# Attention stream: parts of q and k transposed by the DMA engines instead of TensorE, value products grouped by pairs of heads, one block placed earlier

## The chip, the cores and the metric

The kernel runs on one core of a Trainium2 chip. Its time is the device time of one execution in microseconds (us), and the figure compared is the median of several runs. PE is TensorE, ACT is ScalarE, DVE is VectorE, POOL is GpSimd and SP is SyncE, whose queue issues almost all transfers here.

## The reference

```python
# attention: 8 batches, 12 heads, 448 positions, head dimension 64
scores = scale * np.matmul(q, k.transpose(0, 1, 3, 2)) - np.log(S)
attn = 1.0 / (1.0 + np.exp(-scores))
attn_out = np.matmul(attn, v).astype(np.float32)
...
# feed-forward: x is 3584 tokens x 768; w_in is 768 x 2048, w_out is 2048 x 768
x = np.ascontiguousarray(attn_out.transpose(0, 2, 1, 3)).reshape(B * S, H * D)
h = x @ w_in
g = h - np.tanh(h)
return (g @ w_out).astype(np.float32)
```

All inputs are float32. The weights arrive in the kernel as 64-bit words and are converted on the chip.

## The kernel before

A batch of 448 tokens goes through three steps: attention for its 6 pairs of heads, the first product with `w_in` (`moe1`), and the second product with `w_out` (`moe2`). To get float32 accuracy from float16 matmuls, an operand is split into a high and a low float16 part, each with a power-of-two scale, and three products (high·high, high·low, low·high) are summed in PSUM.

Batch 0 is done first with plain float32 matmuls while the weights are loaded and converted. After that attention is a stream (`stream`), a generator that yields one *block* at a time, and the driver `second` places blocks between the steps of a batch's second product. A step is 6 matmuls (`yield 980`), so a batch's second product has 48 steps and 16 half-size ones for the remaining 64 tokens, counted to 56. The tables `BLOCKS0` (batch 0), `BLOCKS1` (batch 1) and `BLOCKS` (later batches) say after which step a block is issued. `ALONE` is the index of the block in `BLOCKS` that completes the next batch's attention. Three, five and seven steps after it come the scales of the next batch's `x` and its splitting into `xhl` (`batch_scales`), which the next `moe1` reads. The first product has no blocks in it.

A pair of heads `g` takes two blocks, `i = 0` and `i = 1`, and each treats two of the four chunks of 112 keys. Before the change a block issues on PE, in this order:

- `i = 0`: four float32 transposes of pair g+1's q through PSUM (`turn`, tile `qT`); `i = 1`: four of pair g+2's k (`turn_k`, tile `kT`) and one small matmul for the sums of squares (line 316);
- 12 score matmuls (line 362), two chunks x three products x two heads;
- 12 products with v (line 386), for the two chunks of the block before (`do_av`).

ACT takes the sigmoid (line 371) and makes the high part of the weights (line 377), DVE the low part (line 378). `parts` splits the transposed q or k, read from PSUM, into `Q` or `K` (lines 337, 339, 340): ACT writes the high part of q, DVE that of k for most pairs, and DVE writes the low part of both. `norms` (line 308) takes sums of squares of a later pair on ACT. The pairs of batch 1 do the v product in float32 instead (`av32`, `AV32 = 2`).

PE, ACT, DVE and POOL run in the order in which the code is written. SP's transfers are placed by the framework's scheduler; SP issues them in order, and each waits there until its source is written and its destination is free. Tiles come from rotating buffers: `K` and `Q` have two buffers each, and so have the loaded `kn` and `qn`.

Of the kernel before, what the change touches and what calls it, by code (L numbers as in the profile page):

```python
# [8 lines left out]
F16 = mybir.dt.float16  # L9
BF16 = mybir.dt.bfloat16  # L10
F32 = mybir.dt.float32
# [3 lines left out]
AF = mybir.ActivationFunctionType  # L15
ALU = mybir.AluOpType
# [3 lines left out]
P = 128  # L20
D = 64
CK = 112
# [12 lines left out]
class Builder:  # L35
# [6 lines left out]

    BLOCKS = (8, 12, 16, 20, 24, 28, 32, 36, 40, 44, 48, 52)
    TAIL = (1, 2, 3, 4, 5)
    ALONE = 8
    BLOCKS0 = (2, 5, 8, 12, 16, 20, 24, 31, 38)
    BLOCKS1 = (4, 7, 10, 13, 16, 19, 22, 25, 28, 32, 36, 40, 44, 48, 52)

    TP = 8
    SHIFT = 4  # L50

    def __init__(self, ctx, tc, q, k, v, w_in, w_out, out):
        self.tc, self.nc = tc, tc.nc
        self.q, self.k, self.v, self.w_in, self.w_out, self.out = q, k, v, w_in, w_out, out
        self.B, self.H, self.S, _ = q.shape
        self.DM, self.DFF = w_in.shape
        self.NP = self.H // 2
        self.NC = self.DM // P
        self.NF = self.DFF // P
        self.HALF = self.DM // 2  # L60
        nc = self.nc
        pool = lambda name, bufs, **kw: ctx.enter_context(tc.tile_pool(name=name, bufs=bufs, **kw))
        self.const = pool("const", 1)
        self.wp = pool("weights", 1)
        self.sm = pool("small", 2)
        self.nat = pool("nat", 2)
        self.qk = pool("qk", 2)
        self.att = pool("att", 2)
        self.xp = pool("xp", 8)
        self.tp = pool("temps", self.TP)  # L70
        self.op = pool("outs", 2)
        self.ps = pool("ps", 1, space=PSUM)

        self.ident = self.const.tile([P, P], F32, name="ident")
        make_identity(nc, self.ident)
        self.onesf = self.const.tile([P, P], F32, name="onesf")
        nc.vector.memset(self.onesf, 1.0)
        self.onesb = self.const.tile([P, P], BF16, name="onesb")
        nc.vector.memset(self.onesb, 1.0)

        self.NB = self.DFF // 256
        self.wi = self.wp.tile([P, self.NC * self.NB + self.SHIFT, 2, 256], F16, name="wi")
        self.wo = self.wp.tile([P, self.NF * 2 + self.SHIFT, 2, self.HALF], F16, name="wo")

    def warm(self, n):

# [25 lines left out]

    def where(self, kind, r, i=0):

        t, n, m = (self.wi, self.NB, 256) if kind == "in" else (self.wo, 1, self.HALF)
        f = t.rearrange("p a b c -> p (a b c)").bitcast(F32)
        r = r * n + i * self.NF + self.SHIFT
        return f[:, r * m : (r + n) * m]

    def conv_load(self, p):  # L120
# [88 lines left out]

    def split(self, t, n, S, act):  # L210

        F = t[:, n + self.SHIFT].rearrange("p b c -> p (b c)").bitcast(F32)
        if act:
            self.nc.scalar.activation(t[:, n, 0], F, AF.Copy, scale=S)  # L214
        else:
            self.nc.vector.tensor_scalar(t[:, n, 0], F, S, None, op0=ALU.mult)
        self.nc.vector.scalar_tensor_tensor(t[:, n, 1], F, S, t[:, n, 0], op0=ALU.mult, op1=ALU.subtract)
# [73 lines left out]
        self.nc.sync.dma_start(t, self.v[b, 2 * j : 2 * j + 2].rearrange("h (p c) d -> p h c d", c=4))  # L291
        return t

    def transpose(self, n, name, tag="tr", bufs=1, t=None):
        nc = self.nc
        if t is None:
            t = self.ps.tile([P, 512], F32, name=name, tag=tag, bufs=bufs)
        for c in range(4):
            nc.tensor.transpose(t[:, c * CK : (c + 1) * CK], n[:, c].rearrange("p h d -> p (h d)"), self.ident[:CK, :CK])  # L299
        return t[:, : self.S]  # L300
# [7 lines left out]
            self.nc.scalar.activation(junk, t.rearrange("p a b d -> p (a b d)"), AF.Square, accum_out=ss[:, i : i + 1])  # L308
        return ss[:, :n]

    def scales(self, ss, pb):

        nc = self.nc
        n = ss.shape[1]
        pb = pb[:, self.S : self.S + n]
        nc.tensor.matmul(pb, self.onesf[:CK, :], ss, start=True, stop=True)
        t = self.sm.tile([P, 3], F32, name="tn")
        nc.scalar.activation(t[:, :n], pb, AF.Relu, bias=self.tiny, scale=2.1)
        y = self.pow2(t[:, :n], n, "n")
        i = self.sm.tile([P, 3], F32, name="in")  # L320
        nc.vector.tensor_scalar(i[:, :n], y, 2.0**49, None, op0=ALU.mult)
        s = self.sm.tile([P, 3], F32, name="sn", bufs=3)
        nc.vector.reciprocal(s[:, :n], i[:, :n])
        r = self.sm.tile([P, 2], F32, name="rn", bufs=5)
        nc.vector.scalar_tensor_tensor(
            r[:, 0:1], i[:, 0:1], 1.0 / math.sqrt(D), i[:, 1:2], op0=ALU.mult, op1=ALU.mult
        )
        if n == 3:
            nc.vector.tensor_scalar(r[:, 1:2], y[:, 2:3], 2.0**49 / A_SCALE, None, op0=ALU.mult)
        return s, r  # L330

    def parts(self, t, s, name, act):

        nc = self.nc
        o = self.qk.tile([P, 2, self.S], F16, name=name, tag=name)
        if act:
            nc.scalar.activation(o[:, 0], t, AF.Copy, scale=s)  # L337
        else:
            nc.vector.tensor_scalar(o[:, 0], t, s, None, op0=ALU.mult)
        nc.vector.scalar_tensor_tensor(o[:, 1], t, s, o[:, 0], op0=ALU.mult, op1=ALU.subtract)  # L340
        return o

    def prep_v(self, vn, s):
# [85 lines left out]
    def stream(self):  # L429
# [5 lines left out]
        G = (self.B - 1) * NP  # L435
        at = lambda g: (1 + g // NP, g % NP)
        splits = lambda g: at(g)[0] >= self.AV32
        qk, v, ss, sc, K, Q, vv = {}, {}, {}, {}, {}, {}, {}
# [8 lines left out]
            if g < G:  # L447
                ss[g] = self.norms(qk[g] + ([v[g]] if splits(g) else []))

        def turn(g, n, name):  # L450
            return self.transpose(qk[g][n], name) if g < G else None

        def turn_k(g):
            if g >= G:
                return None
            t = self.ps.tile([P, 512], F32, name="kT", tag="tr", bufs=1)
            turned = self.transpose(qk[g][0], "kT", t=t)
            sc[g] = self.scales(ss.pop(g), t)
            return turned

        def parts_k(g, t):
            if g < G:
                K[g] = self.parts(t, sc[g][0][:, 0:1], "K", not splits(g) and g not in (2, 3))

        def parts_q(g, t):
            if g < G:
                Q[g] = self.parts(t, sc[g][0][:, 1:2], "Q", True)
                qk.pop(g)

        def prep_v(g):  # L470
# [11 lines left out]
        norms(1)  # L482
        yield 0, False
        for g in range(2):
            parts_k(g, turn_k(g))
            yield 450, False
            parts_q(g, turn(g, 1, "qT"))
            load(g + 2)
            yield 450, False
        norms(2)  # L490
# [4 lines left out]
        def do_av():  # L495
            for g, c, A in todo:
                if c == 0:
                    self.acc = self.ps.tile([P, 512], F32, name="acc", tag="av", bufs=1)
                    if g % NP == 0:
                        self.xs = []  # L500
                (self.av if splits(g) else self.av32)(c, self.acc, vv[g], A)
                if c == 3:
                    self.xs.append(self.evac_x(g % NP, self.acc, sc[g][1][:, 1:2] if splits(g) else None))
                    for d in (sc, K, Q, vv):
                        d.pop(g)
            todo.clear()

        for g in range(G):
            for i in range(2):
                if i:  # L510
                    t = turn_k(g + 2)
                elif g:
                    t = turn(g + 1, 1, "qT")
                pss = [self.scores(c, K[g], Q[g]) for c in (2 * i, 2 * i + 1)]
                aa = [self.weigh(pss[0], sc[g][1][:CK, 0:1])]
                if i:
                    parts_k(g + 2, t)
                elif g:
                    parts_q(g + 1, t)
                aa.append(self.weigh(pss[1], sc[g][1][:CK, 0:1]))  # L520
                do_av()
                if i == 0:
                    if g == 0:
                        prep_v(0)
                    prep_v(g + 1)
                if splits(g):
                    aa = [self.split_a(a) for a in aa]
                todo.extend((g, 2 * i + n, a) for n, a in enumerate(aa))
                if g and i == 0:
                    load(g + 3)  # L530
                elif g:
                    norms(g + 3)
                yield 2750, True
# [350 lines left out]
    def first(self, rest):  # L884
# [16 lines left out]
        next(rest)  # L901
        assert n + len(self.BLOCKS0) + len(self.BLOCKS1) == 4 * self.NP + len(self.BLOCKS) - self.ALONE
        split = self.split_w_in()
# [14 lines left out]
    def batch(self, b):  # L918
# [12 lines left out]
        else:  # L931
            blocks = self.BLOCKS if b + 2 < self.B else self.BLOCKS[: self.ALONE + 1]
        alone = self.ALONE
        if b == 1:
            alone += len(self.BLOCKS1) - len(self.BLOCKS)
            blocks = self.BLOCKS1
# [52 lines left out]
```

## Time and profile before

| | |
|---|---|
| median of 3 runs | 1263.84 us (1262.47 to 1264.2) |
| profiled execution, its own time | 1264.8 us |
| its span in the trace | 1262.5 us |
| granted PE clock over the span | 0.995 of full |
| PE busy | 1235.0 us, 98% |
| DVE busy | 946.7 us, 75% |
| ACT busy | 940.2 us, 74% |

The 2.3 us between the span and the execution's own time lie outside the trace. Busy is the time in which an engine has an instruction in flight. Matmuls overlap one another, so a group's busy time divided by its count is the pace at which they follow, while "mean ns" is how long one is in flight. A row of windows gives the stretch, its length, then the busy time and the instruction count of PE matmuls, PE weight loads, DVE, ACT and POOL, then the granted PE clock, the DMA engines' busy share and GB/s. Rows of windows for one line alone give the engines that it uses.

### The profile page before, as it was taken

To read this page: it belongs to the slowest core of one execution; us is meant where nothing else is said; L and a number is where in the kernel's file an instruction comes from. 1 tells how busy PE (TensorE), PEld (TensorE's weight loads), DVE (VectorE), ACT (ScalarE), POOL (GpSimd) and SP (SyncE) were. 2 spreads that over 40 slices of the span, in tenths; PEclk is the share of its full clock that TensorE was granted. 3 is DMA by queue.
4 is the path that set the end of the run, shared out by engine and by line. 5 is a ranking of instruction groups with operands and counts; after the bars stand their busy time and mean duration, and the time that the engine had idled before them with its cause. 6 is when DMAs were issued, how large, how long until landed. Compare 5 with 4: busy or idle time off the path is not lost.

```text
span 1262.5 us, 20449 instructions
## 1 busy us (share of the span) xinstructions
PE 1235.0 (98%) x8011; PEld 685.3 (54%) x8011; DVE 946.7 (75%) x1473; ACT 940.2 (74%) x1325; POOL 38.6 (3%) x38
## 2 busy tenths in 40 slices
PE   9889889999999999999999999999999999999998
PEld 3245445555556555665555655555556655555555
DVE  5989988789876797676965798667976769645930
ACT  6957788958998688886878688886888868753820
POOL 0100000000010000100000000000000000000000
PEclk9999999999999999999999999999999999999999
DMA  9943254100122101220022200221012200100001
GB/s 261 299 126 90 56 162 136 49 20 1 36 73 57 42 2 42 65 65 7 1 58 64 56 1 16 64 58 41 1 43 67 62 7 1 28 14 20 1 13 32
DMA packets 114367, 70.52 MB, mean 56 GB/s; under 512 B 91872, under 2 KB 104416, under 8 KB 114272
## 3 DMA queue, kind: packets, MB, share of 16 engines
q1 hardware_dynamic: 113344, 69.00, 20.6%
q8 instruction: 63, 1.03, 0.3%
q10 hardware_dynamic: 928, 0.23, 0.1%
q14 instruction: 32, 0.26, 0.1%
HBM read 58.20 MB, written 11.01 MB: 55 GB/s over the span
## 4 chain that ended last, share of the span: by engine, by line
PE 74%; DVE 14%; ACT 6%; issue 3%; DMA 3%; SPq 0%; DVEq 0%; ACTq 0%
PE ph L676 30%; PE po L798 25%; PE sc L362 6%; PE acc L386 5%; PE por L836 3%; DVE ahl L378 2%; ACT a L371 2%; DVE xhl L626 2%; DMA raw<-moe_w_in 1%; PE acc L396 1%; PE qT L299 1%; DVE xhl L625 1%; ACT wo L214 1%; DVE stb L151 1%; DVE m L750 1%
## 5 line engine op out<-in xcount | busy, mean ns | idle before, releaser
L798 PE MATMUL po<-wo,g 128*128 128x384 f16 x2304 | 391.4, 326 | 1.0 <-ACT o L827 1.0
L676 PE MATMUL ph<-xhl,wi 128*128 128x448 f16 x2016 | 382.6, 352 | 0.0
L798 PEld LDWEIGHTS <-g 128*128 128x128 f16 x2304 | 219.5, 98 | 171.3 <-issue 30.4
L676 PEld LDWEIGHTS <-wi 128*128 128x128 f16 x2016 | 196.7, 98 | 185.0 <-issue 1.8
L371 ACT ACTIVATE a<-sc,nls,rn 112x896 f32<-112x896 f32 x168 | 179.9, 1095 | 45.4 <-PE sc L362 38.3
L378 DVE SCALAR_TENSOR_TENSOR ahl<-a,ahl 112x896 f16<-112x896 f32 x144 | 155.7, 1122 | 58.6 <-ACT ahl L377 57.9
L746 ACT ACTIVATE u<-ph,ih 128x896 f32<-128x896 f32 x64 | 64.4, 1006 | 98.9 <-PE ph L676 95.3
L377 ACT ACTIVATE ahl<-a 112x896 f16<-112x896 f32 x144 | 128.0, 939 | 0.0
L362 PE MATMUL sc<-Q,K 64*112 64x448 f16 x1008 | 116.1, 362 | 3.8 <-ACT a L371 2.8
L750 DVE SCALAR_TENSOR_TENSOR m<-ph,ihk,u 128x896 f32<-128x896 f32 x64 | 73.5, 1148 | 54.9 <-ACT th L748 54.6
L386 PE MATMUL acc<-ahl,vhl 112*64 112x448 f16 x864 | 96.4, 357 | 0.5
L660 ACT ACTIVATE g<-m,Sg 128x896 f16<-128x896 f32 x64 | 66.6, 1041 | 34.1 <-DVE m L764 28.7
L764 DVE COPY_PREDICATED m<-u,th 128x896 f32<-128x896 uint32 x64 | 77.3, 1207 | 6.9 <-DVE m L761 0.5
L661 DVE SCALAR_TENSOR_TENSOR g<-m,Sg,g 128x896 f16<-128x896 f32 x64 | 73.4, 1147 | 8.8 <-ACT g L660 8.8
L340 DVE SCALAR_TENSOR_TENSOR Q<-qT,sn,Q 128x448 f16<-128x448 f32 x42 | 28.6, 682 | 67.9 <-ACT Q L337 67.9
L362 PEld LDWEIGHTS <-K 64*112 64x112 f16 x1008 | 60.6, 128 | 32.5 <-issue 6.8
L761 DVE SCALAR_TENSOR_TENSOR m<-q,m 128x896 f32<-128x896 f32 x64 | 69.9, 1093 | 8.3 <-ACT q L760 0.9
L706 PE MATMUL ph<-x,wi 128*128 128x448 f32 x192 | 74.8, 539 | 0.0
L751 DVE SCALAR_TENSOR_TENSOR th<-ph,ih,th 128x896 f32<-128x896 f32 x64 | 73.3, 1145 | 0.0
L763 ACT ACTIVATE u<-u,b 128x896 f32<-128x896 f32 x64 | 66.7, 1043 | 5.6 <-DVE m L750 3.6
L757 DVE SCALAR_TENSOR_TENSOR m<-q,m 128x896 f32<-128x896 f32 x64 | 69.5, 1087 | 0.0
L386 PEld LDWEIGHTS <-vhl 112*64 112x64 f16 x864 | 43.5, 109 | 47.8 <-issue 26.1
(134 smaller groups left out, 1323.0 us busy)
## 6 DMA issues: line engine op xcount, KB each, us to landing
raw<-moe_w_in SPq DMA_DIRECT2D x24, 512.0 KB, 7.5
rawo<-moe_w_out SPq DMA_DIRECT2D x32, 384.0 KB, 3.9
kn<-k SPq DMA_DIRECT2D x96, 112.0 KB, 2.9
vn<-v SPq DMA_DIRECT2D x48, 224.0 KB, 2.7
qn<-q SPq DMA_DIRECT2D x94, 112.0 KB, 2.9
out<-o SPq DMA_DIRECT2D x7, 336.0 KB, 3.1
out<-o SPq DMA_DIRECT2D x7, 288.0 KB, 3.1
out<-o SPq DMA_DIRECT2D x7, 240.0 KB, 2.6
```

The source lines that it names most:

```text
L362: nc.tensor.matmul(ps[:CK, h, :S], K[r, w, cs], Q[r, x, :], start=(n == 0), stop=(n == len(prods) - 1))
L371: nc.scalar.activation(a, ps[:CK, :, :S], AF.Sigmoid, bias=self.nls[:CK], scale=scale)
L377: nc.scalar.activation(A[:, 0], a, AF.Copy, scale=A_SCALE)
L378: nc.vector.scalar_tensor_tensor(A[:, 1], a, A_SCALE, A[:, 0], op0=ALU.mult, op1=ALU.subtract)
L386: nc.tensor.matmul(acc[h * D : (h + 1) * D, : self.S], v[:, w, h, c, :], A[:, x, h], start=(c == 0 and n == 0), stop=(c == 3 and n == 2),)
L661: nc.vector.scalar_tensor_tensor(g[:, 1], m, Sg, g[:, 0], op0=ALU.mult, op1=ALU.subtract)
L676: nc.tensor.matmul(ph[:, e, :S], self.wi[:, c * self.NB + k, part, e * P : (e + 1) * P], xhl[c][:, x, :], start=(i == 0), stop=(i == 3 * s ...
L706: nc.tensor.matmul(ph[:, e, :S], self.where("in", c)[:, f * P : (f + 1) * P], xs[c], start=(c == 0), stop=(c == self.NC - 1),)
L750: V.scalar_tensor_tensor(m, ps, ihk, u, op0=ALU.mult, op1=ALU.mult)
L751: V.scalar_tensor_tensor(th, ps, ih, th, op0=ALU.mult, op1=ALU.subtract)
L764: V.copy_predicated(m, u.bitcast(U32), th)
L798: nc.tensor.matmul(po[i][:, :H], gs[f // 2][:, x, f % 2, tk * P : (tk + 1) * P], self.wo[:, i * self.NF + f, w], start=(f == 0 and n == 0) ...
```

## The change

1. `parts` reads the loaded `kn` or `qn` directly (112 partitions x 512 values) in place of the transposed PSUM tile. It writes high and low part into a new float16 tile `w` (112 x 2 x 512) that has one buffer, and one DMA transpose on SP's queue turns its eight 112x128 blocks into `K` or `Q`. There are 42 pairs, so 84 such transfers. The 336 PE transposes of the stream are gone, and the small matmul of line 316 gets a PSUM tile of its own (`pbn`).
2. `do_av` is called in `i = 0` blocks alone, where the v products are split ones: all 24 v matmuls of a pair then follow one another in the next pair's first block, and an `i = 1` block has none.
3. The tables: batch 0's second product has 10 blocks in place of 9, batch 1's 13 in place of 15, batch 6's 10 in place of 9. From batch 2 on the last block that the next batch needs is the one at step 44, not at 40, so `batch_scales` moves from step 43 to step 47.
4. `wo` is one slot smaller (`SHIFT_O = 3`), which makes room for `w`.

```diff
-    ALONE = 8
-    BLOCKS0 = (2, 5, 8, 12, 16, 20, 24, 31, 38)
-    BLOCKS1 = (4, 7, 10, 13, 16, 19, 22, 25, 28, 32, 36, 40, 44, 48, 52)
+    ALONE = 9
+    BLOCKS0 = (2, 5, 8, 11, 14, 17, 20, 24, 31, 38)
+    BLOCKS1 = (4, 8, 12, 16, 20, 24, 28, 32, 36, 40, 44, 48, 52)
+    SHIFT_O = 3
...
-    def scales(self, ss, pb):
+    def scales(self, ss):
-        pb = pb[:, self.S : self.S + n]
+        pb = self.ps.tile([P, 512], F32, name="pbn", tag="tr", bufs=1)[:, :n]
...
-    def parts(self, t, s, name, act):
+    def parts(self, n, s, name, act):
+        flat = n.rearrange("p c h d -> p (c h d)")
+        w = self.qk.tile([CK, 2, 4 * P], F16, name="w", tag="w", bufs=1)
+        if act:
+            nc.scalar.activation(w[:, 0], flat, AF.Copy, scale=s[:CK])
+        else:
+            nc.vector.tensor_scalar(w[:, 0], flat, s[:CK], None, op0=ALU.mult)
+        nc.vector.scalar_tensor_tensor(w[:, 1], flat, s[:CK], w[:, 0], op0=ALU.mult, op1=ALU.subtract)
         o = self.qk.tile([P, 2, self.S], F16, name=name, tag=name)
-        if act:
-            nc.scalar.activation(o[:, 0], t, AF.Copy, scale=s)
-        else:
-            nc.vector.tensor_scalar(o[:, 0], t, s, None, op0=ALU.mult)
-        nc.vector.scalar_tensor_tensor(o[:, 1], t, s, o[:, 0], op0=ALU.mult, op1=ALU.subtract)
+        nc.sync.dma_start_transpose(
+            o.rearrange("p x (c t) -> p (x c) t", c=4), w.rearrange("p x e -> p (x e)")
+        )
...
             for i in range(2):
                 if i:
-                    t = turn_k(g + 2)
-                elif g:
-                    t = turn(g + 1, 1, "qT")
+                    scales(g + 2)
                 pss = [self.scores(c, K[g], Q[g]) for c in (2 * i, 2 * i + 1)]
...
-                do_av()
+                if i == 0 or not splits(g):
+                    do_av()
```

On PE, at the start of an `i = 1` block in a later batch's second product (`po` is the second product, `sc` the scores), the order before is:

```order
L798 MATMUL po_3887<-wo,g 128x384
L798 LDWEIGHTS g
L798 MATMUL po_3888<-wo,g 128x384
L299 MATMUL kT<-ident,kn 128x112 x4
L316 MATMUL kT<-ss,onesf 128x3
L362 LDWEIGHTS K
L362 MATMUL sc<-Q,K 112x448
L362 LDWEIGHTS K
```

and now:

```order
L796 LDWEIGHTS g
L796 MATMUL po_3058<-wo,g 128x384
L796 LDWEIGHTS g
L796 MATMUL po_3059<-wo,g 128x384
L316 MATMUL pbn<-ss,onesf 128x3
L367 LDWEIGHTS K
L367 MATMUL sc<-Q,K 112x448
L367 LDWEIGHTS K
```

The four transposes are gone, and only the small matmul stands between the second product and the scores.

On SP, in a later batch (`kn`, `qn`, `vn` are loads for later pairs, `out` are stores), the order before is:

```order
L291 DMA vn<-v 112x2x256
L285 DMA kn<-k 112x4x64 x2
L285 DMA qn<-q 112x4x64 x2
L291 DMA vn<-v 112x2x256
L285 DMA kn<-k 112x4x64 x2
L285 DMA qn<-q 112x4x64
```

and now:

```order
L343 DMA_TRANSPOSE K<-w 128x8x112
L286 DMA kn<-k 112x4x64 x2
L343 DMA_TRANSPOSE Q<-w 128x8x112
L286 DMA qn<-q 112x4x64 x2
L292 DMA vn<-v 112x2x256
```

Two transposing transfers per pair now stand in front of loads in the same queue, and each waits for ACT and DVE to have written `w`.

On ACT, in an `i = 0` block (`a` are the sigmoids, `x` the evacuated attention output), the order before is:

```order
L371 ACTIVATE a_11552<-sc,nls,rn 112x896
L337 ACTIVATE Q<-qT,sn 128x448
L371 ACTIVATE a_11557<-sc,nls,rn 112x896
L408 ACTIVATE x_11571<-acc,rn 128x448
L417 ACTIVATE x_11573<-x_11571 128x448
```

and now:

```order
L376 ACTIVATE a_11361<-sc,nls,rn 112x896
L338 ACTIVATE w<-qn,sn 112x512
L376 ACTIVATE a_11368<-sc,nls,rn 112x896
L413 ACTIVATE x_11395<-acc,rn 128x448
L422 ACTIVATE x_11397<-x_11395 128x448
```

The write of the high part keeps its place between the two sigmoids, but its target is now the single buffer `w`, which the transfer of the block before must have read.

## Rows read from the trace of the kernel before

**Rows 1.** The page, part 1: busy us, share of span, instructions.

```profile
PE 1235.0 (98%) x8011; PEld 685.3 (54%) x8011; DVE 946.7 (75%) x1473; ACT 940.2 (74%) x1325; POOL 38.6 (3%) x38
```

**Rows 2.** Windows in batch 1, of batch 2, of one pair: stretch, length, busy us.

```profile
344.00:374.00 30.00, 30.00 (x237) 17.78 (x236) 18.94 (x34) 28.27 (x48) 3.27 (x3) 1.00 0.29 69
424.00:571.00 147.00, 146.89 (x1024) 84.58 (x1022) 111.51 (x166) 116.13 (x159) 4.56 (x4) 1.00 0.15 39
492.85:506.82 13.97, 13.97 (x108) 8.33 (x106) 9.64 (x16) 12.55 (x20) 1.45 (x2) 1.00 0.33 91
```

**Rows 3.** Windows, the transposes of line 299 alone: PE busy, weight loads.

```profile
215.00:1146.00 931.00, 39.83 (x288) 33.71 (x288) 1.00 0.14 36
90.00:215.00 125.00, 7.33 (x48) 5.40 (x48) 0.96 0.38 110
```

**Rows 4.** Windows of the early stretches, all instructions, columns as in 2.

```profile
150.00:180.00 30.00, 24.61 (x147) 11.95 (x146) 26.06 (x52) 28.29 (x47) 0.00 (x0) 0.89 0.41 122
180.00:215.00 35.00, 32.66 (x204) 17.32 (x204) 30.39 (x66) 27.04 (x53) 4.00 (x3) 0.95 0.54 161
```

**Rows 5.** Timeline of PE through one pair in batch 2: start, length.

```profile
492.85 0.55 PE L299 MATMUL kT<-ident,kn 112*128 112x112 f32 x4
493.24 0.30 PE L316 MATMUL kT<-ss,onesf 112*128 112x3 f32 x2
493.46 1.34 PE L362 MATMUL sc<-Q,K 64*112 64x448 f16 x12
494.73 1.33 PE L386 MATMUL acc<-ahl,vhl 112*64 112x448 f16 x12
495.99 4.07 PE L798 MATMUL po<-wo,g 128*128 128x384 f16 x24
499.90 0.55 PE L299 MATMUL qT<-ident,qn 112*128 112x112 f32 x4
500.38 1.34 PE L362 MATMUL sc<-Q,K 64*112 64x448 f16 x12
```

**Rows 6.** The chain that ended last: one run of the first product.

```profile
717.76 54.59 PE ph L676 x288
```

**Rows 7.** Groups by line of DVE and ACT: busy us, mean ns.

```profile
L340 DVE SCALAR_TENSOR_TENSOR Q<-qT,sn,Q 128x448 f16<-128x448 f32 x42 | 28.6, 682 | 67.9 <-ACT Q L337 67.9
L308 ACT ACTIVATE sqn<-kn 112x512 bf16<-112x512 f32 x42 | 26.1, 621 | 0.0
```

**Rows 8.** Timeline of DVE and ACT in blocks: a split from SBUF, the write of Q.

```profile
490.39 0.48 DVE L348 TENSOR_SCALAR vhl<-vn,sn 112x512 f16<-112x512 f32 x1
490.91 0.75 DVE L349 SCALAR_TENSOR_TENSOR vhl<-vn,sn,vhl 112x512 f16<-112x512 f32 x1
...
502.20 0.62 ACT L337 ACTIVATE Q<-qT,sn 128x448 f16<-128x448 f32 x1
...
502.85 0.68 DVE L340 SCALAR_TENSOR_TENSOR Q<-qT,sn,Q 128x448 f16<-128x448 f32 x1 [2.13 <-ACT Q L337]
```

**Rows 9.** DMA: queue with packets, MB, share; issues with KB, us to landing.

```profile
q1 hardware_dynamic: 113344, 69.00, 20.6%
...
kn<-k SPq DMA_DIRECT2D x96, 112.0 KB, 2.9
vn<-v SPq DMA_DIRECT2D x48, 224.0 KB, 2.7
...
out<-oh SPq DMA_DIRECT2D x2, 24.0 KB, 1.9
```

**Rows 10.** Timeline of PE and DVE at the end of batch 3's second product.

```profile
694.79 0.35 PE L603 MATMUL nm<-x2b,onesb 128*128 128x448 bf16 x1
...
708.95 0.15 DVE L630 TENSOR_SCALAR ihk<-ih 128x1 f32<-128x1 f32 x1
...
713.67 4.09 PE L836 MATMUL por<-wo,g 128*64 128x384 f16 x48
717.69 1.50 PE L676 MATMUL ph<-xhl,wi 128*128 128x448 f16 x7
```

More of the change, by code (lines that the diff above doesn't have):

```diff
@@ L82, in __init__ @@
         self.wi = self.wp.tile([P, self.NC * self.NB + self.SHIFT, 2, 256], F16, name="wi")
-        self.wo = self.wp.tile([P, self.NF * 2 + self.SHIFT, 2, self.HALF], F16, name="wo")
+        self.wo = self.wp.tile([P, self.NF * 2 + self.SHIFT_O, 2, self.HALF], F16, name="wo")
     def warm(self, n):
@@ L113, in where @@
     def where(self, kind, r, i=0):
-        t, n, m = (self.wi, self.NB, 256) if kind == "in" else (self.wo, 1, self.HALF)
+        t, n, m, shift = (self.wi, self.NB, 256, self.SHIFT) if kind == "in" else (self.wo, 1, self.HALF, self.SHIFT_O)
         f = t.rearrange("p a b c -> p (a b c)").bitcast(F32)
-        r = r * n + i * self.NF + self.SHIFT
+        r = r * n + i * self.NF + shift
         return f[:, r * m : (r + n) * m]
@@ L210, in split @@
     def split(self, t, n, S, act):
-        F = t[:, n + self.SHIFT].rearrange("p b c -> p (b c)").bitcast(F32)
+        F = t[:, n + (self.SHIFT if t is self.wi else self.SHIFT_O)].rearrange("p b c -> p (b c)").bitcast(F32)
         if act:
@@ L292, in load_v, with transpose @@
         return t
-    def transpose(self, n, name, tag="tr", bufs=1, t=None):
+    def transpose(self, n, name, tag="tr", bufs=1):
         nc = self.nc
-        if t is None:
-            t = self.ps.tile([P, 512], F32, name=name, tag=tag, bufs=bufs)
+        t = self.ps.tile([P, 512], F32, name=name, tag=tag, bufs=bufs)
         for c in range(4):
@@ L448, in norms, with scales, parts_k, parts_q @@
                 ss[g] = self.norms(qk[g] + ([v[g]] if splits(g) else []))
[L450 to L461, printed above, removed]
+        def scales(g):
             if g < G:
-                K[g] = self.parts(t, sc[g][0][:, 0:1], "K", not splits(g) and g not in (2, 3))
-        def parts_q(g, t):
+                sc[g] = self.scales(ss.pop(g))
+        def parts_k(g):
             if g < G:
-                Q[g] = self.parts(t, sc[g][0][:, 1:2], "Q", True)
+                K[g] = self.parts(qk[g][0], sc[g][0][:, 0:1], "K", not splits(g) and g not in (2, 3))
+        def parts_q(g):
+            if g < G:
+                Q[g] = self.parts(qk[g][1], sc[g][0][:, 1:2], "Q", True)
                 qk.pop(g)
@@ L484, in stream @@
         for g in range(2):
-            parts_k(g, turn_k(g))
+            scales(g)
+            parts_k(g)
             yield 450, False
-            parts_q(g, turn(g, 1, "qT"))
+            parts_q(g)
             load(g + 2)
@@ L516, in stream @@
                 if i:
-                    parts_k(g + 2, t)
+                    parts_k(g + 2)
                 elif g:
-                    parts_q(g + 1, t)
+                    parts_q(g + 1)
                 aa.append(self.weigh(pss[1], sc[g][1][:CK, 0:1]))
-                do_av()
+                if i == 0 or not splits(g):
+                    do_av()
                 if i == 0:
```

## The prediction

> **What bounds the kernel now.** I read the page's busy shares first: PE 98%, DVE 75%, ACT 74% [rows 1]. An average can hide stages, so next the windows. Over the whole of batch 2 PE is busy 146.89 of 147.00 us, ACT 116.13 and DVE 111.51; in one pair of heads PE is busy for all of its 13.97 us and ACT for 12.55 [rows 2]. The reader is to see that from about 215 us on PE has no gap, so a microsecond of PE work removed there is a microsecond of time, as long as nothing else becomes later than PE. Before 215 us it is different: from 150 to 180 us PE is busy 24.61 of 30 us at a granted clock of 0.89 while ACT has 28.29, and from 180 to 215 us 32.66 of 35 [rows 4].
>
> **What the removed transposes cost.** Busy time alone would mislead, so I take the distance between starts in a PE that never stops. The q transposes start at 499.90 and the scores behind them at 500.38: 0.48 us. The k transposes start at 492.85, the small matmul at 493.24, the scores at 493.46: 0.61 us for both [rows 5]. The small matmul stays. Behind the transposes its share is 0.61 - 0.48 = 0.13 us; alone, with its weight load uncovered, it may take its full 0.30 [rows 5]. I take 0.21, in the middle, so an i = 1 block saves 0.40, an i = 0 block 0.48.
>
> From 215 to 1146 us lie 288 transposes, 72 sets of four, half of them for k [rows 3]: 36 x 0.48 + 36 x 0.40 = 31.7 us. Their busy time, 39.83 us, is the outer bound, since starts overlap. The other 12 sets stand before 215 us (48 records [rows 3]), where PE is not always the bound. Between nothing and 12 x 0.45 = 5.4 us I take 2.7.
>
> **What the longer runs of v products save.** Twelve score or v matmuls run as six concurrent pairs. The first product moves 448 columns in 54.59 / 288 = 0.190 us [rows 6], so six take 1.14; the run of 12 v products takes 495.99 - 494.73 = 1.26 [rows 5]. The 0.12 difference is paid at each change of kind. A pair now has one run of v products fewer, 36 pairs of batches 2 to 7: 4.3 us. Lower bound nothing, if the 0.12 is spread over the run.
>
> **What is added and moved.** DVE and ACT now read 112 x 512 values from SBUF. The nearest rows are the split of v, 0.48 and 0.75 us for high and low [rows 8], and a sum of squares of the same size on ACT, 0.62 [rows 7]. Before, the write of Q took 0.62 on ACT and its low part 0.68 on DVE [rows 7, 8]. So ACT is unchanged and DVE moves by under 0.1 us per write; DVE is idle 35 of 147 us [rows 2], which hides it. Each transposing transfer adds an entry to SP's queue, behind which loads for later pairs wait. A load lands in 2.9 us [rows 9] and its tile is read about a block later, so 2 or 3 us there are hidden.
>
> Moving a block conserves work: batch 0 takes one more, batch 1 has two fewer, batch 6 one more. Where PE is full, 13 blocks or 15 in a batch add up to the same; in batch 0's start PE has 2.3 us idle in 35 [rows 4], too little to count on. I take nothing.
>
> **The wait that the change adds.** `w` has one buffer. The high part of q on ACT must wait until the transfer of k has landed, and the high part of k until that of q has. Behind ACT's write stand the second sigmoid, the evacuation of x and both high parts of the weights; behind these, the v products and so PE. The cycle of one pair is two writes of `w` and two landings L. By the v split, a k write takes 490.91 - 490.39 + 0.75 = 1.27; a q write 502.85 - 502.20 + 0.75 = 1.40 [rows 8]. Together 2.67 + 2L. The pair on PE will take 13.97 - 0.48 - 0.40 - 0.12 = 12.97 us, so L is hidden up to 5.15 us, and at (13.97 - 2.67) / 2 = 5.65 us the whole gain is gone.
>
> No transposing transfer is in the trace, so I bound L. A transfer moves 112 rows of 2 KB, 224 KB, as much as a `vn` load, which lands in 2.7 us: the lower end. In 256-byte pieces it has 896, twice a `kn` load's, and two of those one after the other take 5.8: the upper end of what rows give. Between them: the whole queue's packets took 20.6% of 16 engines x 1262.5 us for 113344 packets, 37 ns each; 896 / 16 x 37 ns = 2.1 us, on top of the 1.9 us of the smallest store [rows 9]: 4.0 us, which I take. That is hidden with 1.1 us to spare.
>
> On this point the Trainium skill has two rules. The Trainium skill, "Advanced Engine Details and Errata", section "X-Bar Transpose (TRN2)", says that transposing transfers are as fast as ordinary ones; by that L would be 2.7 and the sum stay as it is. The Trainium skill, "VectorE: DVE Perf Modes", section "The three transpose paths", gives 1309 ns for one 128x128 block by DMA against 390 ns on TensorE; an estimate from that page is 8 x 1.309 = 10.5 us for one transfer if its blocks follow one another. No run so far shows either.
>
> **Sum.** 31.7 + 2.7 + 4.3 = 38.7 us, less 1.5 us for new short waits of PE in batch 0, where blocks follow one another three steps apart instead of four and PE already idles 2.3 us in 35 [rows 4] (two thirds of that once more, my choice): about 37 us. The profiled execution took 1264.8 us, 1.0 above the median of 1263.84. From the median: 1227 us.
>
> **Rivals.**
>
> *The single `w` buffer binds (slower).* Decided at L = 5.65 us. At L = 5.8 a pair takes 14.27 us, 0.30 more than before; at 7 us 16.67, 2.70 more. A batch's first pair starts without a backlog, so some 30 pairs count: +9 to +81 us, 1273 to 1345. For it: two `kn` loads in a row are 5.8. Against: the same bytes land in 2.7 [rows 9]. If the eight blocks each pay a small store's 1.9 us, L is 15.2 and a pair 33 us, over 500 us more; the page with 1309 ns per block points that way. Chance of the first 0.17, of the second 0.04. Between 5.15 and 5.65 us the gain is partly eaten, 1230 to 1263: 0.06.
>
> *ACT becomes the bound (little gain).* ACT is busy 12.55 of 13.97 us in a pair [rows 2]; with PE at 12.97 that is 97%. Against it stands batch 1, where blocks are three steps apart: from 344 to 374 us PE is busy 30.00 of 30 us with ACT at 28.27, a pair every 12 us. ACT has thus kept a faster pace than the new one. If it bound at 13.4 us a pair, half the gain of about 1 us over 36 pairs is lost, 1245 us. Chance 0.04.
>
> *The next batch's x is late (smaller gain).* In batch 3 the norms' matmul is at 694.79, the last scale at 708.95, 14.2 us later, and the first product starts at 717.69, 8.7 us after that [rows 10]. With `batch_scales` at step 47 the same work has until: a step, 1.0 us; an i = 1 block, 1.5; 48 half-size matmuls, 4.0; an i = 0 block with 24 v products, 3.7; 48 more, 4.0: 14.2 us, where the half-size runs are 717.69 - 713.67 [rows 10] and the block parts come from [rows 5]. So xhl's last tile is finished as the first product begins, and it is read 15 matmuls, 2.85 us, later. I count it hidden; if DVE is 2 us later than that over five batch ends, the price is up to 10 us: 1237. Chance 0.08.
>
> **How the numbers follow.** The forecast as summed has 0.59, within about 1218 (small matmul free, all early sets counted, outer bounds) and 1238 (no gain from longer runs or early sets); ACT bound 0.04, late x 0.08, gain partly eaten 0.06, slower 0.21; 0.02 for no change by several small waits. Leaving out 0.04 below 1218 and some 0.16 of the slow cases above 1276, the range is 1218 to 1276. Faster by over 0.2% (2.5 us, about what a measurement of this kernel can tell from no change): 0.77; same 0.02; slower 0.21.
>
> **What the profile would show.** Right: no line-299 matmul after batch 0's attention; a pair in batch 2 near 13.0 us with PE full; batch 2 about 6 us shorter than 147; transposing transfers that land in under 5 us; 24 v matmuls in one run. Wrong: ACT idle before the write of `w`, released by the transfer; PE idle before v products; PE idle before `ph` at a batch's first product with DVE `xhl` as the releaser. A landing time above 5.65 us would turn the sign.

## The result and the profile after

The changed kernel takes 1267.35 us in the median of 10 runs (1264.19 to 1268.33), the kernel before 1264.02 (1262.32 to 1266.62) beside it: a ratio of 1.0022, 95% interval 1.0012 to 1.0033. A gain of 37 us was forecast, and a small loss came. The profiled execution took 1267.71 us at a granted clock of 0.984, so 40 us are to be explained against the forecast from the profile, 1264.8 - 37 = 1227.8.

The page, busy us as in [rows 1] and the granted clock in 40 slices; the queue's row and the transfers to set beside [rows 9], each with the median us from issue to landing:

```profile
PE 1211.8 (96%) x7675; PEld 654.2 (52%) x7675; DVE 942.9 (75%) x1473; ACT 943.9 (75%) x1325; POOL 37.9 (3%) x38
...
PEclk9999988999989999999999999999999999999999
...
q1 hardware_dynamic: 191296, 88.28, 29.7%
...
vn<-v SPq DMA_DIRECT2D x48, 224.0 KB, 3.1
...
K<-w SPq DMA_TRANSPOSE x42, 3.0
Q<-w SPq DMA_TRANSPOSE x42, 2.9
```

PE lost 336 instructions and 23 us of work, and yet the span grew: PE now has idle time. ACT and DVE are as they were. The transposing transfers land in 3.0 and 2.9 us, so the single buffer `w`, the first rival, does not bind.

Where the idle time sits shows when the starts of each batch's first product (`ph`) and second product (`po`) are read from PE's timeline and subtracted. This table is worked out from those starts (us):

| stretch | before | changed | difference |
|---|---|---|---|
| batch 0, second product | 170.2 to 266.1 | 169.6 to 276.7 | +11.2 |
| batch 1, first product | 266.1 to 320.6 | 276.7 to 343.3 | +12.1 |
| batch 1, second product | 320.6 to 423.6 | 343.3 to 445.6 | -0.7, two blocks fewer |
| batches 2 to 5, each | 147.0 | 141.8 to 142.6 | about -5.2 |
| batch 6 | 134.9 | 135.8 | +0.9, one block more |
| batch 7, to the end of the span | 115.8 | 115.8 | 0 |

So the steady state gained most of what was forecast for it (5.2 of 6 us a batch), and two places early in the program gave all of it back. The steady state first: windows of batch 2's old place and of the two stretches at the beginning, columns as in [rows 2]:

```profile
424.00:571.00 147.00, 146.41 (x1021) 81.98 (x1019) 113.87 (x170) 121.18 (x170) 4.55 (x4) 1.00 0.26 59
150.00:180.00 30.00, 25.11 (x142) 11.90 (x141) 26.12 (x52) 27.80 (x45) 0.00 (x0) 0.89 0.50 117
180.00:215.00 35.00, 28.84 (x159) 13.24 (x156) 26.94 (x58) 25.82 (x50) 3.43 (x3) 0.90 0.80 209
```

From 424 us PE is full again. From 180 to 215 us it is busy 28.84 us of 35 where it had 32.66 [rows 4], ACT and DVE work less too, and the DMA engines go from 0.54 to 0.80. That points at the transfers, or at the queue in which they stand; it does not tell which, and the experiments try it.

One pair of heads in PE's timeline, as in [rows 5]:

```profile
549.34 4.07 PE L796 MATMUL po<-wo,g 128*128 128x384 f16 x24
553.35 1.34 PE L367 MATMUL sc<-Q,K 64*112 64x448 f16 x12
554.62 2.46 PE L391 MATMUL acc<-ahl,vhl 112*64 112x448 f16 x24
557.01 4.07 PE L796 MATMUL po<-wo,g 128*128 128x384 f16 x24
560.92 0.28 PE L316 MATMUL pbn<-ss,onesf 112*128 112x3 f32 x2
561.13 1.34 PE L367 MATMUL sc<-Q,K 64*112 64x448 f16 x12
562.41 0.50 PE L796 MATMUL po<-wo,g 128*128 128x384 f16 x2
```

From 549.34 to 562.41 are 13.07 us; 12.97 was predicted, from 13.97. The small matmul takes 561.13 - 560.92 = 0.21 us, and the run of 24 v products 557.01 - 554.62 = 2.39, where two runs of 12 took 2.52: these two terms hold. But the pair lost 0.90 us and not 1.00. The rest is in the 24 matmuls of `po` ahead of the scores: they take 553.35 - 549.34 = 4.01 us, where ahead of the q transposes they took 499.90 - 495.99 = 3.91 [rows 5]. So removing a set of q transposes gave back 0.38 us, not the 0.48 between their start and that of the scores.

Now batch 1's first product, which has no block of attention in it. PE's timeline:

```profile
306.29 8.66 PE L674 MATMUL ph<-xhl,wi 128*128 128x448 f16 x36 [2.16 <-DVE th L749]
316.35 6.98 PE L674 MATMUL ph<-xhl,wi 128*128 128x448 f16 x36 [1.39 <-DVE th L749]
326.40 8.67 PE L674 MATMUL ph<-xhl,wi 128*128 128x448 f16 x36 [3.07 <-DVE th L749]
336.47 6.98 PE L674 MATMUL ph<-xhl,wi 128*128 128x448 f16 x36 [1.40 <-DVE th L749]
343.29 4.06 PE L796 MATMUL po<-wo,g 128*128 128x384 f16 x24
...
356.58 1.37 PE L367 MATMUL sc<-Q,K 64*112 64x448 f16 x6 [8.52 <-DVE th L749]
357.87 4.33 PE L391 MATMUL acc<-ahl,vhl 112*64 112x448 f16 x24
```

A group of 36 matmuls now starts every 10.06 us; by [rows 6] it needs 36 x 0.190 = 6.82. PE waits for DVE's `th`, which frees the PSUM tile, and at the end the first scores wait 8.52 us more for the same. DVE, however, is not full. ACT's timeline of one such step, in which `q` is written twice and `g` once, says why:

```profile
307.33 1.04 ACT L754 ACTIVATE q<-u,b 128x896 f32<-128x896 f32 x1 [2.41 <-DVE g L659]
309.53 1.04 ACT L758 ACTIVATE q<-u,b 128x896 f32<-128x896 f32 x1 [1.16 <-DVE m L755]
313.95 1.03 ACT L658 ACTIVATE g<-m,Sg 128x896 f16<-128x896 f32 x1
```

ACT's `q` reads `u` and `b`, neither of which `g` or `m` writes. So it must wait for its own target. The code takes `q` from the pool of temporaries, eight buffers that rotate (`TP = 8`). By the two releasers the first `q` gets the buffer of an earlier step's `m`, which `g` has not yet read to the end, and the second `q` gets that of the first, which DVE's `m` (line 755) is still reading. A step takes five temporaries (`u`, `th`, `m`, two `q`), and `m` is kept for `finish_g` in the next; the chain moves as if it had few buffers. The split weights `ahl` are taken from the same pool. This gave the first theory.

TensorE's granted clock falls as well. The windows are of the second half of the first product, and of the 24 v products behind the 8.52 us of idleness:

```profile
306.00:343.00 37.00, 30.85 (x143) 14.75 (x144) 24.49 (x23) 22.36 (x22) 0.00 (x0) 0.91 0.00 1
357.87:362.13 4.26, 4.26 (x26) 2.00 (x25) 2.18 (x2) 3.07 (x4) 0.00 (x0) 0.55 0.00 0
```

Columns as above, the clock is 0.91 of full in the first, a mix of the two levels of 1.2 and 2.4 GHz, and 0.55 in the second, near the lower level. The 24 v products take 362.13 - 357.87 = 4.26 us (the next row on PE starts at 362.13) in place of 2.39: a wait has cost more than its own length.

### The profile page after: what moved, and what is told of

It is laid out like the page before. It is cut to its first block, busy times and chain, and to the rows that moved or that the text cites. A ratio compares the mean times of both kernels' runs of the same rounds, so it can differ in the third digit from the quotient of the medians.

```text
span 1265.4 us, 19801 instructions
## 1 busy us (share of the span) xinstructions
PE 1211.8 (96%) x7675; PEld 654.2 (52%) x7675; DVE 942.9 (75%) x1473; ACT 943.9 (75%) x1325; POOL 37.9 (3%) x38
## 4 chain that ended last, share of the span: by engine, by line
PE 67%; DVE 15%; ACT 12%; issue 3%; DMA 3%; SPq 1%; DVEq 0%; ACTq 0%
PE ph L674 26%; PE po L796 22%; PE sc L367 6%; PE acc L391 5%; PE por L834 5%; ACT a L376 2%; DVE m L748 2%; DVE m L762 2%; DVE m L759 1%; DVE g L659 1%; DVE m L755 1%; ACT ahl L382 1%; ACT sqn L308 1%; DVE ahl L383 1%; ACT th L746 1%
## 5 line engine op out<-in xcount | busy, mean ns | idle before, releaser
L674 PE MATMUL ph<-xhl,wi 128*128 128x448 f16 x2016 | 386.6, 355 | 8.0 <-DVE th L749 8.0
L391 PE MATMUL acc<-ahl,vhl 112*64 112x448 f16 x864 | 90.5, 360 | 0.0
L341 DVE SCALAR_TENSOR_TENSOR w<-qn,sn,w 112x512 f16<-112x512 f32 x42 | 31.6, 751 | 67.8 <-ACT w L338 67.7
L754 ACT ACTIVATE q<-u,b 128x896 f32<-128x896 f32 x64 | 66.1, 1032 | 16.7 <-DVE g L659 16.7
L758 ACT ACTIVATE q<-u,b 128x896 f32<-128x896 f32 x64 | 66.1, 1032 | 11.0 <-DVE m L755 10.5
```

The source lines that it names most:

```text
L391: nc.tensor.matmul(acc[h * D : (h + 1) * D, : self.S], v[:, w, h, c, :], A[:, x, h], start=(c == 0 and n == 0), stop=(c == 3 and n == 2),)
L674: nc.tensor.matmul(ph[:, e, :S], self.wi[:, c * self.NB + k, part, e * P : (e + 1) * P], xhl[c][:, x, :], start=(i == 0), stop=(i == 3 * s ...
```

## The experiments

**Theories.** R (ring): the pairing holds four `ahl` buffers of the eight whenever a batch's second product ends on an `i = 1` block, whose v products now wait for the next `i = 0` block, which is on the far side of the next first product. The number of blocks that lie ahead decides: batch 0's second product now has 4 + 10 = 14 blocks in place of 13 and ends on `i = 1`; the later ones end on 24 + 3 = 27, an `i = 0`. D (transfers): the added transfers slow the loads of weights and of the next x, everywhere. T (tables): the new places of blocks crowd the early stages. R says that batch 1's loss has nothing to do with the transposes or with where batch 0's blocks are placed; D and T say that it has. In the expectations R is theory 1, and theory 2 is that batch 0 ends late and leaves ACT and DVE a backlog; T is theory A in the later ones.

**The same kernel, with pair 6's products flushed.** `NP` is the number of pairs whose v product is not split, so `g == NP` is the pair with which batch 0's second product ends.

```diff
-                if i == 0 or not splits(g):
+                if i == 0 or not splits(g) or g == NP:
```

> The changed kernel with one more call of do_av, in the i = 1 block that is the last of batch 0's second product, so that two split weight tiles instead of four stay in the eight-buffer ring of temporaries through batch 1's first product. Theory 1 (held buffers): batch 1's first product goes back from 66.6 us to about 54.6, the 8.5 us wait of scores on DVE behind it goes too, total about 1267 - 20 = 1247 us. Theory 2 (batch 1 is slow because batch 0 ends late and ACT and DVE carry a backlog into it): no change, 1267 us.

Measured: 1245.04 us, 0.9842 [0.9818, 0.9867]. PE's timeline of the same place:

```profile
276.36 54.65 PE L674 MATMUL ph<-xhl,wi 128*128 128x448 f16 x288
330.85 4.06 PE L796 MATMUL po<-wo,g 128*128 128x384 f16 x24
```

The first product starts at the same moment, with the same transfers ahead of it, and takes 54.5 us in place of 66.6; ACT's waits for `q` are gone from it. One edit that only sends 12 matmuls earlier gives 22.3 us: for batch 1's loss R holds, and D, T and the backlog do not.

**The same, by the table instead.** Batch 0 gets back its 13 blocks, with the pairing left as it is.

```diff
-    BLOCKS0 = (2, 5, 8, 11, 14, 17, 20, 24, 31, 38)
-    BLOCKS1 = (4, 8, 12, 16, 20, 24, 28, 32, 36, 40, 44, 48, 52)
+    BLOCKS0 = (2, 5, 8, 12, 16, 20, 24, 31, 38)
+    BLOCKS1 = (4, 7, 10, 13, 16, 20, 24, 28, 32, 36, 40, 44, 48, 52)
```

> The changed kernel with the tables of batch 0 as before (9 blocks, so it ends on an i = 0 block) and 14 blocks in batch 1. Theory 1 (held buffers): batch 1's first product at 54.6 us as in e1_flush, and batch 0's second product shorter by the block moved out (2.7 us, which batch 1 gets back) and by part of its new waits: 1240 to 1247 us, at or below e1_flush. Theory 2 (backlog): between 1255 and 1267 us, by what batch 0 gains alone.

Measured: 1245.25 us, 0.9842 [0.982, 0.9864]. Batch 1's first product takes 54.5 us again, with two held buffers by another edit. That the total is the same is in part chance: by the starts, batch 0's second product takes 101.1 us (106.6 in the flushed kernel) and batch 1's 97.2 (89.8), and the moved block explains about 2.7 of each difference.

**No pairing.**

```diff
-                if i == 0 or not splits(g):
+                if True:
```

> The changed kernel with do_av in every block, so no grouping by pairs at all; transposes by DMA and the new tables stay. Theory 1 (held buffers): batch 1's first product at about 54.6 us as in the run before, but 36 runs of v products more at 0.12 us, total about 1251 us. Theory 2 (backlog): 1267 + 4 = 1271 us.

Measured: 1246.42 us, 0.9853 [0.9834, 0.9872]. The ring's loss is gone here too, with 54.5 us for batch 1's first product. Beside the flushed kernel, the pairing gains 1.4 us, and the two intervals overlap; by the starts of batches 2 to 5 it gains 0.4 to 0.5 a batch (142.3 against 141.8 to 142.3), where 0.72 was taken.

**The pairing alone, in the kernel before.** With the old tables 13 + 15 = 28 blocks lie ahead from batch 1 on, so each later second product ends on `i = 1`. If R is right, every later first product must be slow, with no transposing transfer in the kernel.

```diff
-                do_av()
+                if i == 0 or not splits(g):
+                    do_av()
```

> The kernel before with grouping of the v products by pairs alone: PE transposes and old tables stay. With the old tables batch 0 ends on an i = 0 block and batches 1 to 5 end on an i = 1 block. Theory 1 (held buffers): the first products of batches 2 to 6 are slow, about 66 us in place of 54.6 each and a wait behind, some 20 us x 5, total about 1360 us; batch 1's first product stays at 54.6. Theory 2 (backlog from batch 0): no first product slows, and the 36 saved runs give 1264 - 4 = 1260 us.

Measured: 1360.06 us, 1.0756 [1.073, 1.0782]. PE's timeline in batch 2 and then, from the groups of ACT's waits from 420 to 500 us (total us, times, longest), one that matters:

```profile
422.59 27.41 PE L677 MATMUL ph<-xhl,wi 128*128 128x448 f16 x144
452.16 6.98 PE L677 MATMUL ph<-xhl,wi 128*128 128x448 f16 x36 [2.15 <-DVE th L752]
462.23 6.98 PE L677 MATMUL ph<-xhl,wi 128*128 128x448 f16 x36 [3.08 <-DVE th L752]
472.30 6.98 PE L677 MATMUL ph<-xhl,wi 128*128 128x448 f16 x36 [3.09 <-DVE th L752]
```

```profile
ACT q L757 <- DVE g L662: 14.2, 6, 2.4
```

The steps are 10.07 us apart, as in the changed kernel, and ACT's wait on DVE's `g` is the same 14.2 us in six times that the changed kernel shows from 276 to 350 us. By the starts the loss comes five times, 18.5 to 20.5 us a batch with the pairing's small gain in it, and batch 1's first product, behind 13 blocks, takes 54.5. This settles that four `ahl` buffers held over the boundary in place of two cost this, with or without transposing transfers. That they do it through the pool of temporaries is read from ACT's waits and the code; no run gave the pool more buffers.

**The transposing transfers alone**, with the tables of before and no pairing.

```diff
-    ALONE = 9
+    ALONE = 8
...
-    BLOCKS0 = (2, 5, 8, 11, 14, 17, 20, 24, 31, 38)
+    BLOCKS0 = (2, 5, 8, 12, 16, 20, 24, 31, 38)
...
-                if i == 0 or not splits(g):
+                if True:
```

`BLOCKS1` is that of before too.

> The DMA transposes alone: the tables of the kernel before, do_av in every block. By the stages of e3_nopair and e2_tables: batch 0's second product 101 us in place of 96 (+5), batch 1's 15 blocks save 15 x 0.4 us (-6), batches 2 to 5 save 4.6 us each (-18.5), batch 6 3.5 us: total about 1242 us. If what costs batch 0 its 5 us is not the transposes but the new tables or the pairing, batch 0 stays at 96 us and the total is about 1237 us.

Measured: 1252.85 us, 0.9908 [0.989, 0.9925]: 11 us above what was expected. By the starts, batch 0's second product takes 103.1 us against 96.0, with the same 13 blocks at the same places: so a loss of this size comes with the transposes, without the new table. The wait of ACT that grew, in that stage (total us, times, longest; before it was 0.8 in two):

```profile
ACT stb L146 <- DMA rawo<-moe_w_out: 8.0, 3, 6.2
```

`rawo` are the words of `w_out`, still being loaded and converted. Batches 2 to 5 take 143.8 us each, 1.4 more than without pairing in the new tables; PE's recorded waits differ by only 0.5 us a batch (4.7 against 2.3 us in five batches), so that part stays open.

**Why are the words late?** SP's timeline of the changed kernel:

```profile
194.18 1.26 SPq L286 DMA_DIRECT2D kn<-k  x2
196.13 2.30 SPq L343 DMA_TRANSPOSE Q<-w  x1
198.48 1.25 SPq L286 DMA_DIRECT2D qn<-q  x2
199.83 1.51 SPq L131 DMA_DIRECT2D rawo<-moe_w_out  x3
```

Its DVE and ACT beside it:

```profile
195.35 0.75 DVE L341 SCALAR_TENSOR_TENSOR w<-qn,sn,w 112x512 f16<-112x512 f32 x1
...
203.63 0.55 ACT L146 ACTIVATE stb<-rawo 128x384 f32<-128x384 f32 x1 [5.33 <-DMA rawo<-moe_w_out]
```

The transpose of `w` starts at 196.13, just after DVE has finished `w` at 196.10, occupies SP for 2.30 us, and the weight's loads stand behind it; before it SP had issued nothing since 195.44. ACT then waits 5.33 us for them; behind ACT's instruction stand the sigmoids, and behind those PE. Two explanations are left: Q, the queue (loads wait behind a transfer that waits for `w`), and D, the transfers themselves (DMA share 0.84 from 170 to 215 us, 0.60 before). The time that a transfer takes SP to issue is counted with Q in the next expectation and with D in the last.

**The loads on POOL's queue**, for the second half of `w_out` alone, in the flushed kernel.

```diff
-        self.nc.sync.dma_start(p["raw"], src[r * P : (r + 1) * P, i * n : (i + 1) * n])
+        queue = self.nc.gpsimd if i and not p["staged"] else self.nc.sync
+        queue.dma_start(p["raw"], src[r * P : (r + 1) * P, i * n : (i + 1) * n])
```

> e1_flush with the 16 loads of w_out's second half issued from POOL's queue instead of SP's. Theory Q (the transposing transfers, which wait in SP's queue for w to be written and take over 1 us each to issue, hold up the loads behind them): batch 0's second product shrinks from 106.7 us by about 6, total about 1239 us. Theory D (the 16 DMA engines are busy with the transposes' small packets, so the loads land late from any queue) and theory A (ACT and DVE are crowded by blocks three steps apart): no change, 1245 us.

Measured: 1247.19 us, 0.9865 [0.9838, 0.9893], no gain; batch 0's second product took 112.9 us in the profiled execution, where about 101 was expected by Q. The loads land in 5.0 us there and ACT waits 8.1 us for them:

```profile
ACT stb L147 <- DMA rawo<-moe_w_out: 8.1, 2, 4.8
```

POOL too issues in order, each load behind waits of its own (the three at 186.39 us stand behind an addition that waited 15.89 us for ACT's `x`), so this run does not tell Q from D: inconclusive.

**TensorE transposes for the first seven pairs**, as before the change, in the flushed kernel. `parts_pe` is `parts` of before, reading `t`.

```diff
+    EARLY = 7
...
-            if g < G:
+            if g < self.EARLY:
+                K[g] = self.parts_pe(turned.pop(g), sc[g][0][:, 0:1], "K", not splits(g) and g not in (2, 3))
+            elif g < G:
...
```

> e1_flush with the first 7 pairs (all of batch 1's and one of batch 2's) transposed by TensorE as in the kernel before, the rest by DMA. Theories Q and D (the transposing transfers cost batch 0 its time, by their queue or by the engines): batch 0's second product from 106.7 back to about 99 us (96 and one block more), total about 1238 us. Theory A (crowded blocks): no gain, and up to 14 x 0.4 us of PE time back, 1245 to 1250 us.

Measured: 1238.13 us, 0.9796 [0.978, 0.9811], the fastest version, and faster than both kernels. Windows of 170 to 215 us, first of the changed kernel, then of this one, columns as above:

```profile
170.00:215.00 45.00, 37.40 (x213) 17.74 (x212) 36.70 (x81) 35.52 (x67) 3.43 (x3) 0.92 0.84 215
```

```profile
170.00:215.00 45.00, 40.73 (x257) 20.92 (x256) 39.14 (x87) 37.01 (x70) 3.41 (x3) 0.96 0.59 178
```

PE does more transposes and the kernel is 7 us faster by the medians than with the flush alone (5 by the profiled executions): here a transpose on PE cost less than one by DMA. `rawo` is no longer among ACT's waits of 0.5 us or more in this stage. But batch 0's second product still takes 103.9 us, where about 99 was expected. Set beside one another, by the starts, in all runs that do the same work there with the blocks at these places:

| batch 0's second product, us | 13 blocks | 14 blocks |
|---|---|---|
| TensorE transposes | 96.0 (before), 95.8 (pairing alone) | 103.9 (first seven pairs; a few transfers at the end of the stage) |
| DMA transposes | 101.1 (by the table), 103.1 (transfers alone) | 107.2 (changed), 106.6 (flushed), 109.0 (no pairing) |

Runs of the same work differ by up to 2.4 us. The transfers cost 5 to 7 us with 13 blocks and 3 to 5 with 14. The fourteenth block costs 8 us with TensorE transposes, of which its own matmuls and transposes are about 3: PE is not full in this stage, and a block moved into it costs some 5 us beyond its work. A part is 3.2 us in which PE waits for ACT at the norms of the next `x` (`nm`). The new table starts those three steps behind its block at 31, at step 34, where the old one started them at 41; the kernel before has no such wait.

**The blocks spread out** in the flushed kernel (T, theory A).

```diff
-    BLOCKS0 = (2, 5, 8, 11, 14, 17, 20, 24, 31, 38)
+    BLOCKS0 = (2, 5, 8, 12, 16, 20, 24, 28, 32, 38)
```

> e1_flush with batch 0's ten blocks at steps 2, 5, 8, 12, 16, 20, 24, 28, 32, 38: four apart while w_out is converted, with the scales of x at steps 35 to 39 instead of 34 to 38. Theory A (crowded blocks): batch 0's second product about 5 us shorter, total about 1240 us. Theories Q and D: within 2 us of 1245 us.

Measured: 1243.31 us, 0.9834 [0.9818, 0.9849]. Batch 1 starts 1 us earlier (275.3 against 276.4), but the stage itself is not shorter: it began at 167.2 and takes 108.1 us against 106.6. PE's waits for the norms are gone, and those of `sc` for ACT's sigmoids are 6.8 us where they were 2.8. So the distance between the blocks is not the cause; that the stage holds one block more remains.

**Both together**: the seven early pairs on TensorE and blocks spread, at (2, 5, 8, 12, 16, 20, 24, 28, 33, 38).

> e7_pe_early with batch 0's ten blocks at steps 2, 5, 8, 12, 16, 20, 24, 28, 33, 38 and the scales of x at 36 to 40. In e7_pe_early PE still waited 3.2 us for the norms of x behind ACT in batch 0. If that wait comes from blocks three steps apart (theory A), it goes: about 1235 us. If ACT is simply full in that stretch, 1238 us as before.

Measured: 1241.49 us, 0.9816 [0.9802, 0.983]. No gain over the seven early pairs alone; the norms' wait of 2.3 us went, and another took its place among PE's waits, the small matmul on DVE's write of Q:

```profile
PE pbn L321 <- DVE Q L345: 4.4, 1, 4.4
```

**Q or D: transposes that nobody reads.** The kernel with seven early pairs on TensorE gets transposing transfers of the same size back, of the loaded tile into an unused `w`: they wait for no written `w`, and nobody needs them.

```diff
+        x = self.qk.tile([P, 2, 4 * P], F16, name="w", tag="w", bufs=1)
+        nc.sync.dma_start_transpose(
+            x.bitcast(mybir.dt.uint16).rearrange("p a b -> p (a b)")[:, : 8 * CK].rearrange("p (a b) -> p a b", a=8),
+            n.rearrange("p c h d -> p (c h d)").bitcast(mybir.dt.uint16),
+        )
```

> e7_pe_early, in which TensorE transposes the first 7 pairs, with the 14 transposing transfers of these pairs issued all the same on SP's queue, from the loaded tiles into a tile that nothing reads. They have the size and place of the real ones but do not wait for a written w, and no engine waits for them. Theory D (their issue time and their packets on the DMA engines delay the other transfers): the 5 to 7 us that e7_pe_early gained over e1_flush are lost again, about 1244 us. Theory Q (the damage is done by SP standing still until w is written): 1238 us as e7_pe_early.

Measured: 1241.47 us, 0.9814 [0.9797, 0.9831]. Its window:

```profile
170.00:215.00 45.00, 40.69 (x267) 21.20 (x265) 39.50 (x87) 37.55 (x71) 3.78 (x3) 1.00 0.77 218
```

The DMA share is back at 0.77 and PE, ACT and DVE are as busy as without the idle transfers; `rawo` is not among ACT's waits of 0.4 us or more. When SP issues the weights' loads says more (durations in ns, then first and last start in us): first the changed kernel, then seven early pairs, then this one.

```profile
L131 SPq DMA_DIRECT2D rawo<-moe_w_out x32: 327/406/1437, 43.0 to 208.8; - x32
```

```profile
L132 SPq DMA_DIRECT2D rawo<-moe_w_out x32: 327/334/1366, 42.2 to 200.6; - x32
```

```profile
L132 SPq DMA_DIRECT2D rawo<-moe_w_out x32: 327/378/1573, 40.2 to 201.9; - x32
```

The last load goes out at 208.8 in the changed kernel and at 201.9 here, with the transfers in the same queue. So the weights are late by the standing for `w`, and not by the transfers' issue or packets: Q, for this wait. What it is worth in time is less clear. The stage is 1.5 us shorter than with the early pairs alone (102.3 against 103.9 us), within the spread above, and the profiled execution (1238.23 us) was the fastest of the four. The medians are 3.3 us apart the other way, with intervals that overlap a little, so up to 3 us may be the transfers themselves: that share is not settled.

## Why the prediction was wrong

The profile's account closes. The flushed kernel's profiled execution took 1242.33 us, the changed one's 1267.71: the ring is worth 25.4 us by these (22.3 by the medians). From 1227.8 to 1242.3 are 14.5 us: batch 0's second product and the size of the steady gain, below, to within 0.6 us.

**Moved blocks (the step that failed first).** The prediction said "Moving a block conserves work" and took nothing. Work is conserved, buffers are not. The extra block makes batch 0's second product end on `i = 1`, and the pairing, which was entered as a gain with a lower bound of nothing, then carries four `ahl` buffers through the next first product. No rival had this. Of the 25.4 us, 12.1 lie in the first product and 12.6 in the second (102.3 against 89.8 us): 8.5 in one wait, 1.9 in the v products at low clock, and 1.3 for a run of 12 that the flush sends ahead; about 1 us is not placed. Either edit was harmless for the ring without the other, as two of the runs show: no pairing with the new tables, and pairing with 13 blocks.

**Batch 0's second product (the second).** Two sentences failed here together. "Moving a block conserves work", with nothing taken for it, looked at stages where PE is full; in this one the block costs some 5 us beyond its work. "Each transposing transfer adds an entry to SP's queue, behind which loads for later pairs wait" and "2 or 3 us there are hidden" are right for `kn` and `qn`, and wrong for `rawo`, which the same queue carries in batch 0 and which the sentence did not look at. The stage takes 106.6 us in the flushed kernel against 96.0. A block is about 2.6 us of PE (in the pair above, 1.27 + 2.39 + 0.21 + 1.28 = 5.15 for two), so 8.1 us are loss. Forecast was -2.7 + 1.5 = -1.2, and 1.8 more saved by four of the 72 later sets, which lie in this stage: -3.0. So 11.1 us are missing. Each of the two causes alone costs about 5 us or more, both together 8.1; the runs do not divide it further.

**The size of the steady gain.** From batch 1's first product to batch 7's the flushed kernel needs 847.8 us against 880.6; without the moved block's 2.6 the gain is 30.2 us. In that stretch of the kernel before lie 272 of the transposes of line 299, 68 sets (columns as in [rows 3]):

```profile
266.10:1146.70 880.60, 37.58 (x272) 31.89 (x272) 1.00 0.14 35
```

Forecast for them were 34 x 0.48 + 34 x 0.40 + 4.3 = 34.2 us. So 4.0 us are missing: the mechanism held, a term was too large. The q transposes gave back 0.38 a set in the pair above and not 0.48, 3.4 us over 34. And there is a new wait in batches 2 to 6 of the changed kernel (groups of PE's waits, 430 to 1150 us), which the flushed kernel has as well:

```profile
PE po L796 <- DVE o L826: 3.5, 5, 1.1
```

The two, 6.9 us, are more than is missing, so some other gain is not placed. In all, 11.1 + 4.0 = 15.1 us for the 14.5 that were missing.

**What held.** No line-299 matmul follows batch 0's attention; a pair takes 13.07 us; batch 2 is 5.2 us shorter (6 forecast). The landing time, on which a quarter of the chance hung, is 3.0 and 2.9 us, near the lower bound of 2.7 and under the 4.0 taken. So the rivals of the single buffer fell, and with them the reason for the slow side of the range: that the time lies between 1218 and 1276 is luck, by a mechanism that the range did not contain. ACT did not bind (121.18 of 147 us with PE full; its write of `w` took 0.72 us where 0.62 was taken, hidden), and no wait of `ph` on `xhl` is among PE's waits.

On the landing time the trace decides between the two rules weighed before. The Trainium skill, "Advanced Engine Details and Errata", section "X-Bar Transpose (TRN2)", has transposing transfers as fast as ordinary ones: the trace agrees, 3.0 and 2.9 us beside 3.1 for an ordinary load of the same 224 KB in the changed kernel (2.7 before [rows 9]). The Trainium skill, "VectorE: DVE Perf Modes", section "The three transpose paths", gives 1309 ns for a block, from which 10.5 us was estimated for eight in a row: the trace shows that the eight blocks of one transfer don't pay this one after another.

## What to carry to other kernels

When an edit moves where a consumer stands, list what lives in between: which rotating buffers it holds across the next stage, how many are left there, and whether the count of blocks ahead is odd or even. Such a wait shows as an engine that waits for another engine's read of an unrelated tile, as ACT's `q` on DVE's `g`. Ask too whether the engine whose work is moved is the one that bounds the stage it moves into. When a transfer takes over work from an engine, follow everything that its queue carries at each stage, and not only what it carries in the steady state: where loads were urgent, the old way on the engine was the cheaper, and a version with both (TensorE early, DMA later) is 2% faster than the kernel before.

## What the hardware showed

A DMA transpose inside SBUF of 112 rows of 2 KB landed in 3.0 us, and its issue took 1.22 to 2.93 us of SP's time in the kernel with the transfers alone (all but three at most 1.34), against 1.25 us for two ordinary loads of 112 KB. In the queue's row, 84 transposes added 77952 packets, 928 each, and 9.1 points of the engines' time. After PE had idled 8.52 us, its granted clock was 0.55 over a run of 24 matmuls that began 1.3 us later, which took 4.26 us where it takes 2.39.
